# Attention, mixture of experts and a gated second network on one core: maxima in PSUM and three moves in the order of work

## The chip, the core and the metric

The kernel runs on one core of a Trainium2 chip. The metric is the device time of one execution in microseconds (us), lower is better. Every kernel was run several times, and medians are compared; a profile belongs to one more execution, whose own time stands beside its span. The engines are named as in the profile: PE (TensorE, matmuls; PEld is its loading of weights), DVE (VectorE), ACT (ScalarE), POOL (GpSimd), SP (SyncE, which here only issues transfers). SBUF is the core's working memory, PSUM the eight banks that PE writes to.

## The reference

Causal attention over 4 batches, 12 heads, 448 positions of 64 values; its output, as 1792 tokens of 768 values, goes through a layer of 8 experts of which each token uses one, and then through a dense network with h − tanh(h) between its two products.

```python
scores = where(mask, -1e9, q @ k.T / sqrt(64))
x = softmax(scores) @ v                               # 4 x 12 x 448 x 64 -> 1792 x 768
e = argmax(x @ w_gate); gate = softmax(x @ w_gate)[e]
y = gate * sigmoid(x @ w_output_gate)[e] * (relu(x @ w1[e]) @ w2[e])   # 768 -> 1024 -> 768
h = y @ w_in                                          # 768 -> 2048
out = (h - tanh(h)) @ w_out                           # 2048 -> 768
```

## The kernel before

Nothing is scheduled by a planner: each engine works in the order in which the program is written, with waits on the others where data or buffers demand it. Products that need more than 16 bits are split in a high and a low f16 part (`hi`, `lo`).

**Attention** (loop at L610, to about 245 us) goes over 24 units `u` of two heads, each in six pieces `m` of query rows. For a piece PE writes the scores to a PSUM bank with tag "s" (`s_mm`, L323 to L325; three such banks in turn), DVE takes the negated maximum of each row (`s_max`, L333) into an SBUF tile `nm`, multiplies it by 0.125 into `nb` (`s_nb`, L341), and ACT makes exp with `nb` as bias (`s_exp`, L347). A bank is written again when the exp of the piece three before has read it. PE then transposes the result (L365), DVE or ACT copies it out (`t_out`, L371, L373), and PE multiplies with V (L384). Pieces 0 and 1 hold both heads of a unit at once, so that their maxima have two columns; the four others have one. K, Q and V of two units at a time are loaded and split: POOL forms the low parts (L297, L301), and transfers on the SP queue put them in place (L295, L296, L298, L300); POOL issues one load of a pair (L286).

In the units 5 to 15 a chunk `k` of the first expert's raw w1 is converted on the side (`conv1`): ACT makes the high part, POOL the rest, and then `load_raw(1, 0, k)` (L104, SP queue) loads the same chunk of the second expert's w1, 512 KB, in its place.

**The experts** follow, to about 584 us. While the slots of one expert run (`slot`, in steps `z`), the pieces of the next one's weights are converted (`fill_hi`, `fill_lo`; L112, L116, L120). Beside the second expert, `order_a(2)` (L1029, L1037 on DVE) builds an operand and `order_b` (L1056 on PE) multiplies with it, to get the order in which blocks of tokens are handed on.

**The last network** has five groups of token blocks (3, 3, 3, 3, 2). Its loop at L1282 goes over positions `n`, 16 to a group. A position has 18 matmuls (`a_mm`, L1214) into one of two PSUM buffers, then a row of DVE, ACT and POOL operations (`act_a` to `act_d`, L1222 to L1250); the first of these (L1222) empties the buffer. From position 17 on, the second product of the group before runs between them. At n = 9, 10, 11 of group one, the blocks of group two are transposed (`prep2`: PE L148, DVE L150), and right behind each `prep3` makes a small product (PE L1025) that spreads the token scales over the partitions, which ACT copies out (L1026). At n = 12 to 15 SP loads the output weights (`wo_load`, L950); the second of these writes where `prep3`'s operands lie.

Of the kernel before, what the change touches and what calls it, by code (L numbers as in the profile page):

```python
# [12 lines left out]
F32 = mybir.dt.float32  # L13
# [5 lines left out]
ALU = mybir.AluOpType  # L19
AX = mybir.AxisListType  # L20
# [3 lines left out]
B, H, S, D = 4, 12, 448, 64  # L24
# [32 lines left out]
def build(ctx: ExitStack, tc: tile.TileContext, kq0, kq, v, wg, wo, w1, w2, wf, out):  # L57
# [45 lines left out]
    def load_raw(e, x, k, n=1):  # L103
        nc.sync.dma_start(out=(raw1, raw2)[x][:, k : k + n, :], in_=(w1, w2)[x][e, :, k : k + n, :])  # L104
# [73 lines left out]
    with ExitStack() as actx:  # L178
# [133 lines left out]
        def s_mm(u, m):  # L312
            d = st_[u]
            qa, kh, kl = d["t"][0:3]
            hl = (u % 2) * 2
            ps = ps_s.tile([128, 512], F32, tag="s", name=f"s_{u}_{m}")
            i = units[m][0][0]
            n = CP * (i + 1)
            vw = ps[:CP, 0 : len(units[m]) * n].rearrange("p (h n) -> p h n", n=n)
            d["s", m] = vw  # L320
            for z, (_, j) in enumerate(units[m]):
                q = qa[:, hl + j, i * CP : (i + 1) * CP]
                nc.tensor.matmul(out=vw[:, z, :], lhsT=q, rhs=kh[:, hl + j, 0:n], start=True, stop=False)  # L323
                nc.tensor.matmul(out=vw[:, z, :], lhsT=q, rhs=kl[:, hl + j, 0:n], start=False, stop=False)
                nc.tensor.matmul(out=vw[:, z, n - CP : n], lhsT=identb[:CP, :CP], rhs=maskb, start=False, stop=True)  # L325

        def s_max(u, m):
            d = st_[u]
            i, j = units[m][0]
            c0 = 2 * i + j  # L330
            c1 = c0 + len(units[m])
            nm, nb = d["nm"], d["nb"]
            nc.vector.tensor_reduce(out=nm[:, c0:c1], in_=d["s", m], op=ALU.max, axis=AX.X, negate=True)  # L333

        def s_nb(u, m):
            d = st_[u]
            i, j = units[m][0]
            c0 = 2 * i + j
            c1 = c0 + len(units[m])
            nm, nb = d["nm"], d["nb"]  # L340
            nc.vector.tensor_scalar(out=nb[:, c0:c1], in0=nm[:, c0:c1], scalar1=0.125, scalar2=None, op0=ALU.mult)  # L341

        def s_exp(u, m):
            d = st_[u]
# [253 lines left out]
        def conv1(k, z):  # L598
            raw, hi, lo = raw1[:, k], wts0[0][:, 0, k], wts0[0][:, 1, k]
            if z < 2:  # L600
                h = slice(512 * z, 512 * (z + 1))
                scaled("a", hi[:, h], raw[:, h])
            else:
                rest_of("p", lo, raw, hi)
                load_raw(1, 0, k)

        FIRST_T = (NU + 1, 2)
        FILL = {(NU + 1, 4): 1, (NU + 2, 0): 1, (NU + 2, 2): 1, (NU + 2, 4): 1, (NU + 3, 0): 1, 1: 2, 2: 3}
# [2 lines left out]
        for u in range(NU + 5):  # L611
            if ok(u):
                if u % 2 and 3 <= u < 15:
                    load_raw(0, 0, u // 2 - 1)
                if u in (8, 10, 12, 14):
                    load_raw(0, 1, u // 2)
                if u == NU - 2:
                    [load_raw(0, 1, k, 2) for k in range(0, 4, 2)]
                if u == 0:
                    loads[1] = load_unit(1)  # L620
                if u == 1:
                    nc.vector.tensor_scalar(out=wgc[:, :, 0 : 2 * E], in0=wgf, scalar1=WS, scalar2=None, op0=ALU.mult)
                    nc.vector.scalar_tensor_tensor(out=wgc[:, :, 2 * E :], in0=wgf, scalar=WS, in1=wgc[:, :, 0 : 2 * E], op0=ALU.mult,
                                                   op1=ALU.subtract)
                st_[u] = {
                    "t": loads[u // 2][0],
                    "P": at.tile([128, 2, 1120], F32, tag="P", name=f"P_{u}")[:CP],
                    "nm": sm.tile([CP, 8], F32, tag="nm", name=f"nm_{u}"),
                    "nb": sm.tile([CP, 8], F32, tag="nb", name=f"nb_{u}"),
                }  # L630
            if ok(u - 1):
                st_[u - 1]["PT"] = at.tile([CP, 5, 448], F32, tag="PT", name=f"PT_{u - 1}")
            for m in range(6):
                if (u, m) == (0, 5):
                    load_32(2)
                for x, part in zip(START, loads[0][1]):
                    if x == (u, m):
                        part()
                if ok(u) and (m, u % 2) in RS and u // 2 + 1 < 3 * B:
                    loads[u // 2 + 1][1](RS.index((m, u % 2)))  # L640
                if ok(u):
                    s_mm(u, m)
                if m < 5 and ok(u - 1):
                    t_mm(u - 1, m)
                if m == 0 and ok(u - 1):
                    s_exp(u - 1, 5)
                if m > 0 and ok(u):
                    s_exp(u, m - 1)
                if m < 5 and ok(u - 1):
                    t_out(u - 1, m)  # L650
                if m == 5 and ok(u - 3):
                    g_mm(u - 3)
                if m == 1 and ok(u - 4):
                    g_lg(u - 4)
                if ok(u - 2):
                    for z in VM[m]:
                        v_mm(u - 2, *VO[z])
                if ok(u):
                    s_max(u, m)
                if m == 0 and ok(u - 3):  # L660
                    v_out(u - 3, 1, 0)
                if m == 1 and ok(u - 3):
                    v_out(u - 3, 1, 2)
                if m == 3 and ok(u - 2):
                    v_out(u - 2, 0, 0)
                if m == 4 and ok(u - 2):
                    v_out(u - 2, 0, 2)
                if m == 2 and ok(u - 4):
                    g_add(u - 4)
                if m == 2 and ok(u - 3):  # L670
                    x_out(u - 3)
                if m == 3 and NU > u - 3 >= XO:
                    x_store(u - 3)
                if u == 4 and m == 0:
                    wts0 = w_tiles(0)
                if u % 2 and 5 <= u < 17 and 2 <= m < 5:
                    conv1((u - 5) // 2, m - 2)
                for k in CONV.get((u, m), ()):
                    pieces(wts0, [(1, k, *(("a", "v") if k in (2, 3) else ("p", "p")))], 1)
                if u == NU - 1 and m == 0:  # L680
                    t = spare_p("x_first")
                    x_first.extend((t[:, 0 : 2 * DM], t[:, 2 * DM : 2 * DM + F1], t[:, 2 * DM + F1 : 2 * DM + 2 * F1]))
                if (u, m) == FIRST_T:
                    slot_xT(x_first[0], "n0", ps_t)
                    s0 = slot0()
                if (u, m) in FILL:
                    fill0(FILL[u, m])
                if (u, m) == (NU + 2, 0):
                    lctx.close()
                    w16s[1][0] = w16p("w16b1")  # L690
                    wts1 = w_tiles(1, (0,))
                if (u, m) == (NU + 2, 2):
                    w1_next((0,), (0,))
                if (u, m) == (NU + 2, 5):
                    w1_next((1, 2), ())
                if ok(u) and (m, u % 2) == LD and u // 2 + 2 < 3 * B:
                    loads[u // 2 + 2] = load_unit(u // 2 + 2)
                if ok(u):
                    s_nb(u, m)
                if m == 0 and ok(u - 3):  # L700
                    v_out(u - 3, 1, 1)
                if m == 3 and ok(u - 2):
                    v_out(u - 2, 0, 1)
                if ok(u - 4) and (u - 4) % 6 == 5 and m == 2:
                    route = routing((u - 4) // 6)
                if route is not None and (m % 2 == 0 or u >= SLOW):
                    if u - 4 < NU - 1:
                        if next(route) is not None:
                            route = None
                    elif m >= 2:  # L710
                        for weight in route:
                            pass
                        route = None
# [363 lines left out]
    for e in range(E):  # L1077
# [7 lines left out]
        if e + 1 < E:  # L1085
# [10 lines left out]
            def fill_lo(z, e=e):  # L1096
                if e == 0 and z >= 2:
                    next(tl, None)
                pieces(wts[e + 1], PLANS[e][z], e + 2, False)
                if e == 1 and z > 1:  # L1100
                    order_a(z) if z < 3 else order_b()

            fill = (fill_hi, fill_lo)
        else:
# [177 lines left out]
    for n in range(NF + 3):  # L1282
        g, f = divmod(n, KF2)
        if okf(n):
            a_mm(n)
            if n in (9, 10, 11):
                prep2(1, (9, 10, 11).index(n))
                prep3(1, (9, 10, 11).index(n))
            act_a(n)
        if n == 0:  # L1290
            prep1(1, 0, GB[1], False)
# [82 lines left out]
```

## Time and profile before

| | |
|---|---|
| three runs, us | 1056.37, 1058.24, 1058.36 (median 1058.24) |
| the profiled execution, us | 1055.79 |
| its span in the profile, us | 1054.1 |
| mean granted PE clock | 0.982 of full speed |
| busy, us: PE, PEld | 993.4 (94%), 750.0 (71%) |
| busy, us: DVE, ACT, POOL | 801.2 (76%), 597.7 (57%), 471.1 (45%) |
| moved by transfers | 174.93 MB, 166 GB/s over the span |

A timeline row gives the start of an instruction from the beginning of the span, its length, the engine, the line of the program and the operation with its output and inputs; in brackets stands how long the engine was idle before it and whose end it waited for. A row with x18 is 18 such instructions in a row. `DVEq` and `SPq` are the queues' own instructions. Idle time of an engine counts only if a later end hangs on it.

### The profile page before, as it was taken

How to read it: one execution, taken by the hardware profiler on the slowest of the kernel's cores; microseconds unless marked ns; L12 is line 12 of the kernel's file. 1: busy time of each engine (PE TensorE's matmuls, PEld its weight loads, DVE VectorE, ACT ScalarE, POOL GpSimd, SP SyncE). 2: the span in 40 equal slices, each digit the busy share in tenths (PEclk: the TensorE clock that was granted, in tenths of full speed). 3: DMA queues.
4: the chain of work that ended last, by engine and by line, in shares of the span. 5: the costliest groups of instructions: out<-in, count | busy, mean ns of one | idle time of the engine just before them, and what ended most of it. 6: DMA issues, size and time to landing. Idle time of an engine off the chain costs nothing. (4 is left out here: it accounts for less than half of the span.)

```text
span 1054.1 us, 24122 instructions
## 1 busy us (share of the span) xinstructions
PE 993.4 (94%) x9189; PEld 750.0 (71%) x9189; DVE 801.2 (76%) x1609; ACT 597.7 (57%) x1195; POOL 471.1 (45%) x501
## 2 busy tenths in 40 slices
PE   5999999998989999999979879999999999999996
PEld 4999899996867878677856546666666666667763
DVE  7768878786777778778758889888889798786640
ACT  4787776764446266563323578655556566564530
POOL 5476775585111012102227788655544444443321
PEclk9999999999999999999999989999999999999998
DMA  8899998743988878977986605000001000000000
GB/s 246 214 244 298 265 271 210 196 139 113 323 336 302 341 269 321 360 285 251 318 291 231 267 1 215 24 31 23 16 31 38 16 23 16 16 16 16 16 23 23
DMA packets 62833, 174.93 MB, mean 166 GB/s; under 512 B 8400, under 2 KB 23376, under 8 KB 59584
## 3 DMA queue, kind: packets, MB, share of 16 engines
q1 hardware_dynamic: 56352, 147.20, 42.0%
q0 software_dynamic: 6304, 25.63, 8.2%
q8 instruction: 80, 1.31, 0.5%
q14 instruction: 97, 0.79, 0.2%
HBM read 133.09 MB, written 29.62 MB: 154 GB/s over the span
## 5 line engine op out<-in xcount | busy, mean ns | idle before, releaser
L1265 PE MATMUL fo<-wo,g 128*128 128x384 f16 x1344 | 228.2, 326 | 0.0
L1214 PEld LDWEIGHTS <-raw 128*128 128x128 f16 x1440 | 141.8, 99 | 91.2 <-issue 13.7
L1265 PEld LDWEIGHTS <-g 128*128 128x128 f16 x1344 | 131.2, 98 | 83.8
L1224 POOL TENSOR_TENSOR V<-cu,cc 128x384 f32<-128x384 f32 (+1 forms) x80 | 78.8, 985 | 192.5 <-ACT cu L1223 191.8
L161 PEld LDWEIGHTS <-w 128*128 128x128 f16 x2592 | 151.0, 100 | 13.8 <-issue 12.7
L173 PE MATMUL py<-w,hh 128*128 128x384 f16 x544 | 133.8, 328 | 5.6 <-ACT hh L168 5.5
L1214 PE MATMUL fh<-cu,raw 128*128 128x384 f16 (+1 forms) x864 | 134.4, 312 | 4.5 <-DVE cc L1222 4.5
L347 ACT ACTIVATE P<-s,nb 112x112 f32<-112x112 f32 (+1 forms) x192 | 90.2, 496 | 59.3 <-DVE rs L398 29.2
L384 PE MATMUL o<-v,PT 112*112 112x65 f32 x960 | 114.9, 259 | 0.0
L384 PEld LDWEIGHTS o<-v,PT 112*112 112x112 f32 x960 | 105.7, 178 | 0.2 <-ACT xt L406 0.2
L801 POOL DMA_INDIRECT xg<-xs_d,idx x24 | 25.7, 1070 | 173.2 <-issue 38.8
L120 DVE SCALAR_TENSOR_TENSOR w<-raw,w 128x768 f16<-128x768 f32 (+1 forms) x99 | 99.1, 1060 | 2.0 <-ACT w L112 2.0
L112 ACT ACTIVATE w<-raw 128x768 f16<-128x768 f32 (+2 forms) x106 | 89.2, 906 | 16.6 <-ACTq L871 10.4
L1223 ACT ACTIVATE cu<-cc 128x384 f32<-128x384 f32 (+1 forms) x80 | 40.1, 502 | 101.5 <-DVE cc L1222 101.4
L1222 DVE TENSOR_TENSOR cc<-fh,co 128x384 f32<-128x384 f32 (+1 forms) x80 | 42.1, 526 | 68.2 <-PE fh L1214 55.0
L1227 POOL TENSOR_TENSOR X<-cc,X 128x384 f32<-128x384 f32 (+1 forms) x80 | 91.4, 1142 | 4.4 <-ACT cu L1228 0.5
L173 PE MATMUL py<-w,hl 128*128 128x384 f16 x272 | 89.5, 329 | 2.2 <-DVE hl L169 2.2
L333 DVE TENSOR_REDUCE nm<-s 112x2 f32<-112x224 f32 (+1 forms) x144 | 77.2, 536 | 13.5 <-PE s L325 12.1
L1234 DVE SCALAR_TENSOR_TENSOR V<-cu,V 128x384 f32<-128x384 f32 (+1 forms) x80 | 85.2, 1065 | 0.1
L173 PEld LDWEIGHTS <-hh 128*128 128x128 f16 x544 | 52.2, 98 | 38.9 <-ACT hh L168 6.9
L161 PE MATMUL ph<-xT_n,w 128*128 128x128 f16 x1152 | 69.5, 225 | 9.2 <-issue 2.1
L1242 DVE TENSOR_TENSOR V<-V,co 128x384 f32<-128x384 f32 (+1 forms) x64 | 77.8, 1216 | 0.0
(431 smaller groups left out, 1951.1 us busy)
## 6 DMA issues: line engine op xcount, KB each, us to landing
raw<-w SPq DMA_DIRECT2D x48, 512.0 KB
raw<-w SPq DMA_DIRECT2D x60, 384.0 KB
cu<-wf SPq DMA_DIRECT2D x22, 1024.0 KB
wb_d<-co SPq DMA_DIRECT2D x22, 512.0 KB
raw<-kq SPq DMA_DIRECT2D x11, 896.0 KB
ys_d<-yo SPq DMA_DIRECT2D x17, 384.0 KB
raw<-wb_d SPq DMA_DIRECT2D x8, 768.0 KB
xs_d<-xq SPq DMA_DIRECT2D x24, 224.0 KB
```

What stands on the lines that cost most here:

```text
L112: nc.scalar.activation(out=out, in_=in_, func=AF.Copy, scale=WS)
L120: nc.vector.scalar_tensor_tensor(out=out, in0=in_, scalar=WS, in1=hi, op0=ALU.mult, op1=ALU.subtract)
L161: nc.tensor.matmul(out=ph[:, (f % 4) * 128 : (f % 4 + 1) * 128], lhsT=w[0][:, ww, k, f * 128 : (f + 1) * 128], rhs=xTs[tag][:, xx, k, :], ...
L173: nc.tensor.matmul(out=py[:, 0:384], lhsT=hx[:, k, :], rhs=w[1][:, ww, k, z * 384 : (z + 1) * 384], start=(k == 0 and n == 0), stop=(k == ...
L347: nc.scalar.activation(out=d["P"][:, j, OFF[i] : OFF[i] + n], in_=d["s", m][:, z, :], func=AF.Exp, bias=d["nb"][:, 2 * i + j : 2 * i + j + ...
L384: nc.tensor.matmul(out=po[:, i, :], lhsT=d["PT"][:, g, o : o + CP], rhs=d["t"][3][:, hl, j, :], start=(j == 0), stop=(j == i))
L1214: nc.tensor.matmul(out=ph[:, 0:nt], lhsT=wi[ww][:, f // 4, k, f % 4 * 128 : (f % 4 + 1) * 128], rhs=yy[:, k, 0:nt], start=(q == 0), stop=( ...
L1224: nc.gpsimd.tensor_tensor(out=d["V"], in0=d["U"], in1=d["h"], op=ALU.mult)
L1227: nc.gpsimd.tensor_tensor(out=d["X"], in0=d["h"], in1=d["X"], op=ALU.subtract)
L1234: nc.vector.scalar_tensor_tensor(out=d["V"], in0=d[f"S{z}"], scalar=QD[z - 1], in1=d["V"], op0=ALU.add, op1=ALU.mult)
L1242: nc.vector.tensor_tensor(out=d["V"], in0=d["V"], in1=rs_y(g, nt), op=ALU.mult)
L1265: nc.tensor.matmul(out=po[:, 0:384], lhsT=t[:, x, k, i * 128 : (i + 1) * 128], rhs=wo_[ww][:, k, z * 384 : (z + 1) * 384], start=(k == 0 a ...
```

## The change

It has four parts. The row maxima are no longer written to the SBUF tile `nm` but to columns 448 and 449 of the PSUM bank that holds the scores, which these do not use; `s_nb` reads them there. The six loads of the second expert's w1 are issued at the start of units 18 to 23 instead of behind each conversion. `order_a(2)` is written one step of the slot loop sooner. The small products of group two are made at n = 12 (two) and n = 13 (one).

```diff
 def s_mm(u, m):
             d["s", m] = vw
+            d["nm", m] = ps[:CP, S : S + len(units[m])]
 def s_max(u, m):
-            i, j = units[m][0]
-            c0 = 2 * i + j
-            c1 = c0 + len(units[m])
-            nm, nb = d["nm"], d["nb"]
-            nc.vector.tensor_reduce(out=nm[:, c0:c1], in_=d["s", m], op=ALU.max, axis=AX.X, negate=True)
+            nc.vector.tensor_reduce(out=d["nm", m], in_=d["s", m], op=ALU.max, axis=AX.X, negate=True)
 def s_nb(u, m):
-            nm, nb = d["nm"], d["nb"]
-            nc.vector.tensor_scalar(out=nb[:, c0:c1], in0=nm[:, c0:c1], scalar1=0.125, scalar2=None, op0=ALU.mult)
+            nc.vector.tensor_scalar(out=d["nb"][:, c0:c1], in0=d["nm", m], scalar1=0.125, scalar2=None, op0=ALU.mult)
...
 def conv1(k, z):
                 rest_of("p", lo, raw, hi)
-                load_raw(1, 0, k)
...
                 if u in (8, 10, 12, 14):
                     load_raw(0, 1, u // 2)
+                if NU - KD <= u:
+                    load_raw(1, 0, u - NU + KD)
                 if u == NU - 2:
                     [load_raw(0, 1, k, 2) for k in range(0, 4, 2)]
...
-                    "nm": sm.tile([CP, 8], F32, tag="nm", name=f"nm_{u}"),
...
             def fill_lo(z, e=e):
                 pieces(wts[e + 1], PLANS[e][z], e + 2, False)
-                if e == 1 and z > 1:
-                    order_a(z) if z < 3 else order_b()
+                if e == 1 and z in (1, 3):
+                    order_a(2) if z == 1 else order_b()
...
             if n in (9, 10, 11):
                 prep2(1, (9, 10, 11).index(n))
-                prep3(1, (9, 10, 11).index(n))
+            for i in {12: (0, 1), 13: (2,)}.get(n, ()):
+                prep3(1, i)
             act_a(n)
```

NU is 24 and KD is 6. The lines of the changed program stand four lower from L341 on, so L1029 and L1025 below are L1025 and L1021 there.

The queue of SP in the units 21 to 23, before. `xs_d<-xq` stores a unit's result, `raw<-kq` and `raw<-v` load K, Q and V, `kh`, `qa`, `kl` are the copies of their parts, `raw<-w` of 128x1536 the first expert's w2.

```order
L295 DMA kh_3216<-t_11_3219 64x1792 x2
L296 DMA qa_3215<-t_11_3219 64x1792
L298 DMA qa_3215<-lo_3218 64x896
L300 DMA kl_3217<-lo_3218 64x896 x2
L298 DMA qa_3215<-lo_3218 64x896
L300 DMA kl_3217<-lo_3218 64x896 x2
L423 DMA xs_d<-xq_3500 112x4x256
L104 DMA raw_90<-w 128x768
L104 DMA raw_90<-w 128x1536 x2
L423 DMA xs_d<-xq_3664 112x4x256
```

And in the changed kernel:

```order
L295 DMA kh_3192<-t_11_3195 64x1792 x2
L296 DMA qa_3191<-t_11_3195 64x1792
L298 DMA qa_3191<-lo_3194 64x896
L300 DMA kl_3193<-lo_3194 64x896 x2
L104 DMA raw_89<-w 128x1024
L298 DMA qa_3191<-lo_3194 64x896
L300 DMA kl_3193<-lo_3194 64x896 x2
L419 DMA xs_d<-xq_3476 112x4x256
L104 DMA raw_90<-w 128x768
L104 DMA raw_89<-w 128x1024
L104 DMA raw_90<-w 128x1536 x2
L419 DMA xs_d<-xq_3640 112x4x256
```

Two of the loads of 128x1024 are to be seen here, one before the second half of the copies and one between the w2 loads; the rest stands in the same order.

DVE at the end of the second expert's step z = 1, before. `w_2<-raw` are conversions of the next weights, `xT_n` the copy of a transposed slot, `cc` the operand of the ordering matmuls, `order` their result.

```order
L116 TENSOR_SCALAR w_2_8270<-raw_90 128x768
L150 COPY xT_n_85<-pt_I-8512_8513 128x768
L120 SCALAR_TENSOR_TENSOR w_2_8269<-raw_89,w_2_8269 128x1024
L120 SCALAR_TENSOR_TENSOR w_2_8270<-raw_90,w_2_8270 128x768 x3
L1029 TENSOR_TENSOR cc<-pb,io 112x224
L1037 TENSOR_TENSOR cc<-cc,pcs 112x1120
L120 SCALAR_TENSOR_TENSOR w_2_8270<-raw_90,w_2_8270 128x768 x5
L1059 TENSOR_REDUCE smt<-order 128x14
L1060 TENSOR_REDUCE smt<-order 128x14
```

And in the changed kernel:

```order
L120 SCALAR_TENSOR_TENSOR w_2_8245<-raw_89,w_2_8245 128x1024 x4
L1025 TENSOR_TENSOR cc<-pb,io 112x224
L1033 TENSOR_TENSOR cc<-cc,pcs 112x1120
L116 TENSOR_SCALAR w_2_8246<-raw_90 128x768
L150 COPY xT_n_85<-pt_I-8490_8491 128x768
L120 SCALAR_TENSOR_TENSOR w_2_8245<-raw_89,w_2_8245 128x1024
L120 SCALAR_TENSOR_TENSOR w_2_8246<-raw_90,w_2_8246 128x768 x8
L1055 TENSOR_REDUCE smt<-order 128x14
L1056 TENSOR_REDUCE smt<-order 128x14
```

The two rows that write `cc` stand before the conversion and the copy of `xT_n`, and the conversions behind them are in one run.

PE at positions 9 and 10 of the last network, before, one row for each run of matmuls with one output. `pt` are transposes of a block, `rsp` the small product, `fh` the 18 matmuls of a position.

```order
L148 MATMUL pt_I-38658_38659<-identh,wo_34361 128x128
...
L148 MATMUL pt_I-38667_38668<-identh,wo_34361 128x128
...
L1025 MATMUL rsp_I-38676_38677<-wo_34361,onesb 128x256
...
L1214 MATMUL fh_38695<-cu_4971,raw_89 128x384
...
L148 MATMUL pt_I-38714_38715<-identh,wo_34361 128x128
...
L148 MATMUL pt_I-38723_38724<-identh,wo_34361 128x128
...
L1025 MATMUL rsp_I-38732_38733<-wo_34361,onesb 128x256
...
L1214 MATMUL fh_38751<-cu_4971,raw_89 128x384
```

And in the changed kernel, positions 9 to 12:

```order
L148 MATMUL pt_I-38634_38635<-identh,wo_34337 128x128
...
L148 MATMUL pt_I-38643_38644<-identh,wo_34337 128x128
...
L1210 MATMUL fh_38667<-cu_4947,raw_89 128x384
...
L148 MATMUL pt_I-38686_38687<-identh,wo_34337 128x128
...
L148 MATMUL pt_I-38695_38696<-identh,wo_34337 128x128
...
L1210 MATMUL fh_38719<-cu_4947,raw_89 128x384
...
L148 MATMUL pt_I-38738_38739<-identh,wo_34337 128x128
...
L148 MATMUL pt_I-38747_38748<-identh,wo_34337 128x128
...
L1210 MATMUL fh_38771<-cu_4947,raw_89 128x384
...
L1021 MATMUL rsp_I-38790_38791<-wo_34337,onesb 128x256
...
L1021 MATMUL rsp_I-38794_38795<-wo_34337,onesb 128x256
...
L1210 MATMUL fh_38815<-cu_4947,raw_89 128x384
```

Transposes and position matmuls now follow each other, and the first two small products stand together behind position 12's matmuls.

## Rows read from the trace of the kernel before

**Rows 1.** Windows: us, busy of PE PEld DVE ACT POOL, clock, DMA, GB/s.

```profile
55.00:245.00 190.00, 186.24 (x2149) 179.47 (x2147) 151.65 (x477) 140.18 (x342) 131.97 (x151) 1.00 0.84 228
...
637.00:1038.00 401.00, 401.00 (x2630) 253.10 (x2628) 306.26 (x520) 229.60 (x468) 189.55 (x181) 1.00 0.09 32
```

**Rows 2.** Timeline of PE, 21 to 26 us (start, length, operation, [idle, releaser]).

```profile
21.71 0.30 PE L323 MATMUL s<-kh,qa 128*112 128x336 f16 x1 [1.43 <-ACT P L347]
...
23.21 0.35 PE L323 MATMUL s<-kh,qa 128*112 128x448 f16 x1 [0.62 <-ACT P L347]
...
25.29 0.30 PE L323 MATMUL s<-kh,qa 128*112 128x112 f16 x1
```

**Rows 3.** Timelines of DVE, POOL and ACT at the start of attention.

```profile
9.17 0.75 DVE L341 TENSOR_SCALAR nb<-nm 112x2 f32<-112x2 f32 x1
...
19.00 2.02 DVE L341 TENSOR_SCALAR nb<-nm 112x2 f32<-112x2 f32 x1
...
19.12 1.87 POOL L297 TENSOR_TENSOR lo<-raw,t 128x896 f16<-128x896 f32 x1
...
21.05 0.60 ACT L347 ACTIVATE P<-s,nb 112x112 f32<-112x112 f32 x2 [3.27 <-DVE nb L341]
```

**Rows 4.** Groups of DVE to 245 us (busy us, mean ns); one line's semaphores.

```profile
L341 DVE TENSOR_SCALAR nb<-nm 112x2 f32<-112x2 f32 x48 | 26.5, 551 | 1.0
...
L341 DVE TENSOR_SCALAR nb<-nm 112x1 f32<-112x1 f32 x96 | 14.4, 150 | 1.1
...
L395 DVE TENSOR_SCALAR rs<-o 112x4 f32<-112x4 f32 x48 | 7.3, 152 | 1.3 <-PE o L384 1.3
...
L341 DVEq EVENT_SEMAPHORE  x2: 21/21/21, 35.0 to 43.5; - x2
```

**Rows 5.** Timelines of SP's and POOL's transfer issues, 12 to 24 us.

```profile
17.83 0.59 SPq L296 DMA_DIRECT2D qa<-t  x1
...
19.49 1.64 SPq L300 DMA_DIRECT2D kl<-lo  x2
...
22.43 0.60 POOL L286 DMA_DIRECT2D t<-kq  x1 [0.85 <-DMA qa<-t]
```

**Rows 6.** PE, DVE and ACT, 299 to 304 us; window 304 to 306.

```profile
302.64 0.71 PE L1056 MATMUL order<-cc,co 112*128 112x70 bf16 x16 [3.68 <-DVE cc L1037]
...
300.76 0.38 DVE L1029 TENSOR_TENSOR cc<-pb,io 112x224 bf16<-112x224 f32 x1
...
301.25 1.32 DVE L1037 TENSOR_TENSOR cc<-cc,pcs 112x1120 bf16<-112x1120 bf16 x1
...
299.93 0.80 ACT L152 ACTIVATE xT_n<-pt_I-8503_8504 128x768 f16<-128x768 f16 x1
...
304.00:306.00 2.00, 2.00 (x21) 2.00 (x20) 2.00 (x4) 0.78 (x2) 0.00 (x0) 0.50 1.03 420
```

**Rows 7.** Timelines of PE and DVE, 625 to 652 us.

```profile
625.79 0.37 PE L1025 MATMUL rsp_I-38676_38677<-wo,onesb 128*128 128x256 bf16 x1 [3.93 <-DVE yh L150]
...
625.95 5.64 PE L1214 MATMUL fh<-cu,raw 128*128 128x384 f16 x18
...
632.68 3.09 PE L1214 MATMUL fh<-cu,raw 128*128 128x384 f16 x18
...
651.49 0.81 PE L1214 MATMUL fh<-yh,raw 128*128 128x384 f16 x4
...
631.97 0.56 DVE L150 COPY yh<-pt_I-38714_38715 128x768 f16<-128x768 f16 x1 [2.72 <-PE pt_I-38714_38715 L148]
...
647.00 0.55 DVE L1222 TENSOR_TENSOR cc<-fh,co 128x384 f32<-128x384 f32 x1
...
650.42 0.55 DVE L1222 TENSOR_TENSOR cc<-fh,co 128x384 f32<-128x384 f32 x1
```

**Rows 8.** Timeline of SP's issues near 198 us, and of PE at 207 us.

```profile
198.25 1.49 SPq L300 DMA_DIRECT2D kl<-lo  x2
...
207.69 0.21 PE L323 MATMUL s<-kh,qa 128*112 128x112 f16 x1
```

## The prediction

> **What bounds the kernel now.** I read the profile from the outside in. First come the busy times by stage [rows 1]: TensorE (PE) is to be seen at 401.00 of 401 us in the long last stage and at 186.24 of 190 in the body of attention. So a microsecond taken off VectorE (DVE), ScalarE (ACT) or a queue counts only where PE stands still. Next come the orders of time around each place that the edits touch, to find who ended PE's wait there: the start of attention [rows 2, 3], and further down the ordering step of the second expert and the scale products of group two in the last stage. Since PE has no gap from 637 us on, time saved before that stage should reach the end. The profiled execution took 1055.79 us, 2.45 under the median of the three runs (1058.24). I sum against 1055.79 and take the difference from the median. A change under 0.2%, about 2.1 us, can't be told from none.
>
> **Part 1, the row maxima in PSUM.** Of the 144 short multiplications that turn a maximum into the bias of exp, the 96 with one column take 150 ns and the 48 with two columns take 551 ns [rows 4]. One of the long ones is to be seen in [rows 3]: it runs from 19.00 to 21.02, and a GpSimd (POOL) operation runs from 19.12 to 20.99, so both end together; ACT's exp then starts at 21.05 after 3.27 us idle. A DVE operation of nearly the same shape that reads PSUM took 152 ns in each of 48 cases, beside the same POOL work [rows 4]. So I price the new reading at 152 ns: the 19.00 one shrinks by 1.87 us, the 9.17 one by 0.60.
> Writing the maximum to PSUM instead of SBUF has no row of its own. The nearest rows are the short operations of 150 ns, so the bounds are one of these more or less, 0.15 us, 0.9 us over the six reductions of a unit. I take 0, since the reduction works on PSUM already and the 152 and 150 ns lie so close.
> The diff's order also has 78 more semaphore instructions on DVE, 21 ns each [rows 4], 1.6 us in all. They lie beside PE's work: DVE is 151.65 of 190 us busy there [rows 1]. The extra wait of the reductions is for an exp that PE had to wait for before it wrote the same bank, so it has ended.
> What reaches PE: in [rows 2] PE waits 1.43 and 0.62 us for that late exp, and the chain before it may give the 0.60 us of the 9.17 operation. That makes 2.65 us at most, whatever the reductions gain, for PE has no more to give up there. Against it stands the next thing that is late: the copies of the low parts of K for the second pair of units are issued until 21.13, and the nearest copy whose landing shows was issued by 18.42 and landed at 22.43, 4.0 us [rows 5]. If these take as long they land at 25.1, and PE wants them at 25.29 [rows 2], so only 0.2 us would come off; if they take half as long, 2.2. I take 1.5 us, nearer to the short landing because each of these copies is half as large as that one (64x896 against 64x1792 in the orders of the queue), and keep 0.2 to 2.65. In the rest of attention PE is busy 98% of the time, so I take nothing, with 1 us either way.
> [...]
>
> **Part 2, the second expert's first weights.** Six loads of 512 KB leave the places after the conversions of units 5 to 15 and stand at the start of units 18 to 23: on the SP queue the first four go ahead of copies of K and Q, the last two ahead of nothing but weights. Nothing uses them before expert 1. Bytes and instructions stay the same. At 228 GB/s [rows 1] one takes 2.3 us of the transfer engines. The last pair's copies are issued until 199.74, and PE wants the first half at 207.69 [rows 8], 7.95 us later. Two loads (4.6 us) ahead of a copy of up to 4.0 us come to 8.6 in the worst case, 0.7 us over; two pairs, 1.4 us. In the units that the loads leave, each pair carried this much and more, and PE still was busy 98% of the time. I take 0, and keep 1.4 as the bound.
>
> **Part 3, the operand of the ordering step.** Two DVE operations, 0.38 and 1.32 us, move from behind five conversions of weights and a copy of transposes to before them. PE waits 3.68 us for the second of them, until 302.64 [rows 6]. When it no longer waits for DVE, the next to be late is the PSUM buffer, which the ACT copy frees at 299.93 + 0.80 = 300.73. So PE starts 1.9 us sooner. What they are moved past comes 1.7 us later and is for the slots after the ordering matmuls; nothing else waits on DVE there. After the gap PE ran at half its clock (0.50 from 304 to 306), and a shorter gap of 1.8 us may let it fall less. What a whole fall costs is to be seen in [rows 7]: 18 matmuls took 5.64 us instead of 3.09, 2.55 us. Bounds 0 and 2.55; I take 0.8, since the gap is halved and not gone. Together 2.7, bounds 1.9 and 4.45.
>
> **Part 4, the scale products.** PE stands 3.93 us before the first product because DVE, behind two blocks of activation work, has not yet copied the transposes out [rows 7]. Then 18 matmuls take 5.64 us at half clock, so the next transposes come late and DVE waits 2.72 us for them, at 631.97. In the changed order the three products stand two to three positions later, so PE goes from the transposes at 621.9 straight on. The wait of 3.93 and the 2.55 of clock do not both come off: behind them PE is paced by DVE, whose work of one position takes 3.42 us (647.00 to 650.42) against PE's 3.09. The sum goes by DVE: its 2.72 us of waiting vanish, all that follows moves up by that, and the operation at 650.42 comes at 647.70 and ends at 648.25. The matmuls of position 17 need its buffer; they started at 651.49 and may start at 648.25: 3.2 us. The three products cost PE what they did, 0.37 us or less each. Their copies on ACT, two of them now at one position, lie in ACT's waits for DVE, the slower engine; without that cover they would be a rival (below). The load of the output weights on SP that writes where the last product's operand lies is now held until position 13, near 639 (632.68 and two positions); it is wanted behind position 17, 651.49. Bounds: 2.7 (DVE's wait alone) and 3.9 (PE's whole wait). I take 3.2.
>
> **The sum.** 1.5 + 0 + 2.7 + 3.2 = 7.4 us. Against the profiled execution 1055.79 − 7.4 = 1048.4, against the median 1058.24 − 7.4 = 1050.8. With the bounds of the parts the gain is 1.5 to 12 us (least: 0.2 − 0.9 − 1 − 1.4 + 1.9 + 2.7; most: 2.65 + 1 + 4.45 + 3.9).
>
> **The rivals.**
> The start gives nothing, because the copies of the second pair land at 25.1 or because the two-column operation also stalls on PSUM. For it speaks the 4.0 us of [rows 5], against it the 48 readings without a stall [rows 4]. Gain 5.9, time 1052.3.
> In the last stage PE's wait only moves: it waits for DVE position by position, and the later products push back ACT as well, which leaves 0.8 of the 3.2. For it speaks that DVE is the slower of the two there. Gain 5.0, time 1053.2.
> The clock stays up as well at the start, where PE is slowed after its waits; a whole fall there is again 2.55 us. Gain 9.9, time 1048.3.
> The reading of PSUM costs more than that of SBUF. The nearest row that a slower one could follow is 150 against 152 ns, so nothing; a third more, 50 ns, is 0.3 us of the first chain: 1051.1. [...]
> Two of the three gains are swallowed by the next wait: about 2 us are left, 1056.
> **Slower:** the moved loads hold up the last K and Q copies. It decides where these land later than 7.95 us after issue [rows 8]. Were the 4.6 us of two loads exposed whole in both late pairs, with a fall of the clock each time (2.55), that would be 14.3 us lost, less 7.4 gained: 6.9 slower, 1065.1. Against it speaks that the same queue carried the same loads earlier without holding PE.
>
> **How the numbers follow.** Forecast 0.50; the start gives nothing 0.15; the wait only moves 0.12; the clock as well 0.08; dearer PSUM reading 0.03; two swallowed 0.08; slower 0.04. All but the last two are faster by over 0.2%: 0.88. Two swallowed is within 0.2%: 0.08. The predicted time is the forecast's, 1050.8. The range reaches down past the case with the clock (1046.5) and up to just short of two swallowed (1055.5).
>
> **What would show it.** The two-column multiplication in the changed profile means about 150 ns, none at 2 us; the exp at 21.05 comes near 19.2, and the waits of 1.43 and 0.62 us are gone. The ordering matmuls wait under 2 us, released by ACT or by nothing. The scale products wait for nothing; short waits of the position matmuls for DVE appear between 626 and 650, and the 18 matmuls take about 3 us. No wait of PE stands at the first score matmuls of units 20 to 23. It would be wrong if the two-column mean stays near 550, if a wait of several us for a copy of K or Q appears near 190 or 208, or if PE has a gap after 637 us that the old trace has not.

## The result and the profile after

The change took 1047.03 us in the median of 4 runs (1044.79 to 1049.29) against 1058.24 in the median of three of the kernel before; a fourth run of that one, 1075.49 us, was in a slower state and is not compared. The ratio is 0.9899 with a 95% interval of 0.9868 to 0.9930, so 7.4 to 14.0 us less. The forecast was 1050.8, 7.4 us less, with a range of 1046.5 to 1055.5. Two later series gave 0.9910 (0.9875 to 0.9944) and 0.9888 (0.9847 to 0.9930). Single executions of one kernel lie several us apart: 35 of the kernel before, on one chip, went from 1051.43 to 1061.87, and 25 on another from 1053.12 to 1068.26. Much of that goes with PE's clock, 0.990 at the fastest and 0.979 at the slowest of the 35, 0.988 and 0.976 of the 25: whether it falls behind a short gap differs from one execution to the next. Behind a wait of 1.47 us for one exp of attention it stayed at 1.00 in the kernel before; behind 1.79 us for the same exp, in another kernel, it went to 0.50. The profiled execution of the change is the slowest of its four, 1049.29 us with a span of 1047.6.

The windows of the change, with the columns of [rows 1]:

```profile
55.00:245.00 190.00, 189.15 (x2196) 181.82 (x2195) 143.03 (x492) 143.49 (x345) 131.38 (x150) 1.00 0.87 234
...
637.00:1038.00 401.00, 400.32 (x2623) 252.41 (x2621) 300.62 (x511) 224.56 (x459) 185.91 (x177) 1.00 0.09 31
```

PE is busy 189.15 us of the body of attention where it was 186.24, and DVE has 8.6 us less to do there. The last stage is nearly as full as it was: PE stands 0.68 us in it, in two waits of 0.34 us for DVE before the positions 16 and 17. Short waits for DVE were forecast there; a gap after 637 us that the old trace has not was also named as a sign of being wrong, and by the letter these two are that.

The groups of DVE to 245 us, as [rows 4]:

```profile
L337 DVE TENSOR_SCALAR nb<-s 112x1 f32<-112x1 f32 x96 | 14.8, 154 | 1.1
...
L337 DVE TENSOR_SCALAR nb<-s 112x2 f32<-112x2 f32 x48 | 7.6, 159 | 0.9
```

The two-column operation takes 159 ns where it took 551; that is 18.9 us of DVE. The longest of all 144 is 161 ns. The one of unit 1 runs right beside POOL, whose subtraction holds from 19.55 to 21.43 (first DVE, then POOL, then PE and SP, at the start):

```profile
19.58 0.16 DVE L337 TENSOR_SCALAR nb<-s 112x2 f32<-112x2 f32 x1
...
19.55 1.88 POOL L297 TENSOR_TENSOR lo<-raw,t 128x896 f16<-128x896 f32 x1
...
20.67 0.35 PE L324 MATMUL s<-kh,qa 128*112 128x448 f16 x1 [0.41 <-ACT P L343]
...
22.80 0.23 PE L324 MATMUL s<-kh,qa 128*112 128x112 f16 x1 [0.67 <-ACT PT L369]
...
23.52 0.26 PE L325 MATMUL s<-kl,qa 128*112 128x112 f16 x1 [0.50 <-DMA kl<-lo]
...
19.91 1.66 SPq L300 DMA_DIRECT2D kl<-lo  x2
```

Of the waits of 1.43 and 0.62 us of [rows 2], 0.41 is left, and unit 2 begins at 22.80 instead of 25.29. It begins behind a wait of 0.67 for an ACT copy, and then the transfer that was named as next to be late does come late: PE waits 0.50 us for the low part of K, until some 2 us after its issue.

The ordering step and the scale products, on PE:

```profile
296.07 0.70 PE L1052 MATMUL order<-cc,co 112*128 112x70 bf16 x16 [2.10 <-ACT xT_n L152]
...
617.90 0.50 PE L148 MATMUL pt_I-38634_38635<-identh,wo 128*128 128x128 f16 x6
...
619.62 3.09 PE L1210 MATMUL fh<-cu,raw 128*128 128x384 f16 x18 [0.89 <-DVE cc L1218]
...
623.60 3.08 PE L1210 MATMUL fh<-cu,raw 128*128 128x384 f16 x18
...
641.57 2.11 PE L1210 MATMUL fh<-yh,raw 128*128 128x384 f16 x12 [0.34 <-DVE cc L1218]
```

The ordering matmuls wait 2.10 us instead of 3.68 [rows 6], and for ACT. The sign named was a wait under 2 us: this one lies just over it. The position behind the transposes takes 3.09 us instead of 5.64 [rows 7], with a wait of 0.89 in place of 3.93.

### The profile page after: what moved, and what is told of

Same layout as the page of the kernel before. It is cut to its first block, busy times and chain, and to the rows that moved or that the text cites. A ratio compares the mean times of both kernels' runs of the same rounds, so it can differ in the third digit from the quotient of the medians.

```text
span 1047.6 us, 24204 instructions
## 1 busy us (share of the span) xinstructions
PE 991.2 (95%) x9189; PEld 748.4 (71%) x9189; DVE 783.1 (75%) x1609; ACT 596.9 (57%) x1195; POOL 471.3 (45%) x501
## 5 line engine op out<-in xcount | busy, mean ns | idle before, releaser
L1210 PE MATMUL fh<-cu,raw 128*128 128x384 f16 (+1 forms) x864 | 132.1, 308 | 6.6 <-DVE cc L1218 6.6
L330 DVE TENSOR_REDUCE s<-s 112x2 f32<-112x224 f32 (+1 forms) x144 | 78.9, 548 | 15.5 <-PE s L326 14.3
```

The lines of the kernel that those rows point to most:

```text
L330: nc.vector.tensor_reduce(out=d["nm", m], in_=d["s", m], op=ALU.max, axis=AX.X, negate=True)
L1210: nc.tensor.matmul(out=ph[:, 0:nt], lhsT=wi[ww][:, f // 4, k, f % 4 * 128 : (f % 4 + 1) * 128], rhs=yy[:, k, 0:nt], start=(q == 0), stop=( ...
```

## The experiments

All are compared with the kernel before in their own series; ratios of runs are coarse here, so each profile was also measured in stretches, between the starts of the same PE instructions. In the table, A is the start of unit 4; B goes from there to unit 23; C from the first transposes of rows of tokens (L148, at 258.31 before) to the ordering matmuls; D from these to the next second product of an expert; E from the first transposes of group two (621.03 before) to position 16 (648.56). The row "split bias" is the slowest execution of its series.

| kernel | A | B | C | D | E |
|---|---|---|---|---|---|
| before | 42.53 | 174.30 | 44.33 | 10.88 | 27.53 |
| the change | 40.87 | 170.73 | 42.83 | 9.25 | 23.67 |
| part 1 alone | 40.24 | 171.30 | 44.58 | 10.88 | 26.59 |
| part 2 alone | 40.99 | 176.04 | 44.61 | 10.83 | 26.27 |
| part 3 alone | 40.87 | 172.91 | 41.97 | 9.25 | 27.39 |
| part 4 alone | 41.76 | 178.35 | 44.39 | 10.88 | 23.65 |
| all parts, second series | 40.02 | 177.44 | 43.22 | 10.75 | 23.67 |
| all but part 1 | 42.66 | 174.23 | 42.65 | 9.25 | 23.65 |
| split bias | 40.22 | 181.13 | 44.44 | 10.88 | 27.51 |
| all, free bank | 40.38 | 171.62 | 40.45 | 9.25 | 23.65 |
| part 1 to unit 3 | 40.21 | 176.94 | 43.84 | 10.54 | 26.49 |
| part 1 from unit 4 | 41.76 | 178.61 | 43.89 | 12.03 | 26.60 |
| all parts, third series | 39.91 | 171.49 | 41.74 | 9.25 | 23.64 |
| all, free bank, again | 40.32 | 176.31 | 40.48 | 9.25 | 23.65 |

### The four parts, each alone

Each kernel is the one before with the lines of the diff that belong to one part. Part 1:

```diff
+            d["nm", m] = ps[:CP, S : S + len(units[m])]
-            nc.vector.tensor_reduce(out=nm[:, c0:c1], in_=d["s", m], ...)
+            nc.vector.tensor_reduce(out=d["nm", m], in_=d["s", m], ...)
...
-            nc.vector.tensor_scalar(out=nb[:, c0:c1], in0=nm[:, c0:c1], ...)
+            nc.vector.tensor_scalar(out=d["nb"][:, c0:c1], in0=d["nm", m], ...)
```

> Only the row maxima in PSUM. Theory A (the maxima are the whole gain of attention, since the traces of before and after stand 5.1 us apart at the end of attention): 5 us faster than before, 2.5 of it before unit 2 begins and 2.6 in the body, where PE's waits fall from 3.7 us to under 1. Theory B (the moved weight loads give the body's share, by taking work out of units 5 to 15): 2.5 us faster, with PE's waits between 55 and 245 us still near 3.7. The prediction's own term was 1.5 us.

Measured: ratio 0.9981 (0.9956 to 1.0005) over 12 runs, about 2 us, and not clear of nothing. In its profile attention is done 4.9 us sooner, as theory A has it, with PE's waits between 55 and 245 us at 1.5 us; but that is one execution against one, and over the runs the gain is less than half of it.

Part 2:

```diff
-                load_raw(1, 0, k)
+                if NU - KD <= u:
+                    load_raw(1, 0, u - NU + KD)
```

> Only the second expert's first weights loaded late. Theory A and the prediction: no change, within 1 us, with the two-column bias operations still at 550 ns in the mean. Theory B: 2.6 us faster, PE's waits between 55 and 245 us gone. Rival of the prediction: slower, with a wait of PE for copies of K or Q near 190 or 208 us.

Measured: ratio 1.0000 (0.9978 to 1.0023). The two-column bias operations take 646 ns in the mean and PE's waits between 55 and 245 us are 4.0 us, so theory B falls; so does the rival of the prediction, for in none of the profiles with the late loads has PE a wait for copies of K or Q between 185 and 218 us.

Part 3:

```diff
-                if e == 1 and z > 1:
-                    order_a(z) if z < 3 else order_b()
+                if e == 1 and z in (1, 3):
+                    order_a(2) if z == 1 else order_b()
```

> Only the operand of the ordering step built one position sooner. Prediction: 2.7 us faster (1.9 of wait and 0.8 of clock). The traces of before and after show 3.2 us here, 1.6 of it clock, but 1.4 us of that lost again in the next 25 us; a rival is therefore that the gain of clock is only handed on to a later place, and 1.8 us remain.

Measured: ratio 0.9981 (0.9954 to 1.0007). In its profile C is 2.4 us shorter than before and D 1.6; PE waits 1.1 us before the ordering matmuls, for ACT. The gain of clock isn't handed on to a later place: D ends at the first run of second products behind the ordering matmuls, and to the next such run it is 28.4 us here and 30.07 before, 28.2 to 29.9 in the seven profiles with this part and 29.9 to 32.9 in the seven without, 2.4 us less in the mean.

Part 4:

```diff
-                prep3(1, (9, 10, 11).index(n))
+            for i in {12: (0, 1), 13: (2,)}.get(n, ()):
+                prep3(1, i)
```

> Only the scale products of group two moved. Prediction: 3.2 us faster, from DVE's 2.72 us of waiting and the slack behind it; PE at full clock from 624 to 632 us and 18 matmuls in 3.1 us. Rival: the wait only moves to DVE, 0.8 us faster.

Measured: ratio 0.9969 (0.9937 to 1.0000). E is 23.65 us, in all seven profiles with this part 23.6 to 23.7, and 26.3 to 27.5 in the seven without. Not all of that lasts: position 17 starts 3.43 us behind position 16, with a wait for DVE, where it was 2.93. From the first transposes of group two to the end of the execution it is 429.7 us in all seven with the part and 431.8 to 433.1 in the seven without, 2.8 less in the mean. So the rival, 0.8, falls too. The ratios of the four parts add up to 0.69% less, 7.3 us.

### All parts again, and all but the first

> All four parts, once more and with more runs. If the parts add up as they were measured alone (1.0, 0 and two times about 2 to 3 us), 7 us faster than before, ratio 0.993. If they help each other, as the first measurement of the change says (11 us), ratio 0.990.

Measured: 1050.19 against 1058.23, ratio 0.9910 (0.9875 to 0.9944). Its interval holds both expected values, so this doesn't settle whether the parts help each other. Its profile shows what scatters. Windows at the end of unit 9, with the columns of [rows 1]:

```profile
92.00:94.00 2.00, 0.50 (x4) 0.10 (x2) 1.93 (x7) 1.02 (x3) 1.92 (x4) 1.00 0.83 271
94.00:96.00 2.00, 1.33 (x11) 1.33 (x12) 0.15 (x1) 0.46 (x1) 1.89 (x4) 0.53 0.79 195
96.00:98.00 2.00, 2.00 (x16) 2.00 (x16) 0.32 (x2) 0.98 (x2) 1.83 (x3) 0.50 0.87 172
```

Two waits for POOL's `xq` (1.16 and 1.01 us) stand before a stretch at half clock. Units 9 and 10, which take 8.88 and 9.14 us undisturbed, took 12.39 and 11.09.

The change without its first part is the diff less the lines shown for part 1.

> The change without its first part (maxima in SBUF as before). Theory A, the maxima give 5 us at the end of attention and these are kept to the end: 5 us slower than all four parts together, 3 to 5 us faster than before. Theory B, what attention gains is given back among the experts: within 2 us of all four parts.

Measured: ratio 0.9932 (0.9906 to 0.9957), 7.2 us faster than before and 2.3 slower than all parts in the same series by the ratios. That lies near theory B's edge and speaks against the 5 us of theory A, but the two intervals overlap. Here and in part 1 alone the maxima are worth some 2 us in the whole kernel, and in neither is that clear of nothing.

### What stalls: the form in SBUF

```diff
-            nc.vector.tensor_scalar(out=nb[:, c0:c1], in0=nm[:, c0:c1], scalar1=0.125, ...)
+            for c in range(c0, c1):
+                nc.vector.tensor_scalar(out=nb[:, c : c + 1], in0=nm[:, c : c + 1], scalar1=0.125, ...)
```

> The kernel before, with each two-column bias operation made as two of one column, all in SBUF. Theory A, the stall belongs to the form with two columns in SBUF on both sides: no bias operation over 200 ns, and attention ends about 4 us sooner, though 48 more operations run. Theory C, the stall belongs to any operation of SBUF that runs beside POOL, so that PSUM is what helps: still operations of over 500 ns among them, and attention no shorter.

Measured: ratio 0.9942 (0.9905 to 0.9980). The line's own answer for the bias operations (shortest, median and longest in ns):

```profile
L342 DVE TENSOR_SCALAR nb<-nm x192: 142/153/156, 8.9 to 231.5; 112x1 f32<-112x1 f32 x192
```

None of the 192 stalls, all in SBUF: theory C falls, and the stall belongs to the form with two columns. A is 40.22 us, as short as with PSUM. The expected gain of attention, though, isn't in this profile, which is the slowest execution of its twelve (1062.06 us, the median is 1052.26): B is 181.13, with two units of 11.52 and 14.67 us instead of 8.88 and 9.07, and PE at half clock from 120 to 128 us. Over the runs this kernel is 6.1 us faster than before (2.1 to 10.1), where part 1 alone gave 2.0 (from 0.5 slower to 4.7 faster). The intervals overlap, so it isn't shown that either form is the better one.

### Where part 1 gains: the start or the body

Against part 1 alone:

```diff
-            d["nm", m] = ps[:CP, S : S + len(units[m])]
+            d["nm", m] = ps[...] if u < 4 else d["nm"][...]      # the other kernel: u >= 4
```

> The kernel before, with the maxima in PSUM in units 0 to 3 alone. If the start gives 1.4 us by itself (units 4 begin at 40.4 us in the mean with the maxima in PSUM, at 41.8 without), unit 4 begins near 40.4 us here, and from there to unit 23 it takes 172 us or more as without them, with waits of PE for exp in the units 9 to 20.

> The kernel before, with the maxima in PSUM from unit 4 on alone. Unit 4 begins near 41.8 us as without them. Theory A, the short operations of the body cost PE 2 to 4 us that the prediction set at nothing: unit 4 to unit 23 in about 171 us, unless PE's clock falls once. Rival, the body's length is scatter alone: 172 to 178 us.

Measured: 0.9977 (0.9939 to 1.0015) and 0.9976 (0.9937 to 1.0015). The start is as expected: A is 40.21 with the maxima in PSUM in units 0 to 3, and 41.76 without. The body of the first kernel is as expected too: B is 176.94, with waits of PE for exp of 1.35 and 0.39 us. That of the second is not: from unit 4 on with PSUM, B is 178.61. Both forms stand in one profile of the second kernel:

```profile
L338 DVE TENSOR_SCALAR nb<-s 112x2 f32<-112x2 f32 x40 | 6.4, 159 | 0.7
L338 DVE TENSOR_SCALAR nb<-nm 112x2 f32<-112x2 f32 x8 | 5.8, 726 | 0.3
```

What held PE in this body (DVE, POOL and PE, then the windows):

```profile
104.83 2.40 DVE L505 TENSOR_SCALAR pi<-pi 112x4 int32<-112x4 int32 x1
...
105.32 1.89 POOL L297 TENSOR_TENSOR lo<-raw,t 128x896 f16<-128x896 f32 x1
...
109.26 0.30 PE L325 MATMUL s<-kh,qa 128*112 128x336 f16 x1 [1.79 <-ACT P L344]
...
110.00:112.00 2.00, 2.00 (x15) 1.86 (x13) 1.90 (x9) 2.00 (x9) 0.79 (x2) 0.58 0.94 326
112.00:114.00 2.00, 2.00 (x13) 2.00 (x12) 1.17 (x4) 1.62 (x4) 1.97 (x3) 0.50 0.21 56
```

An integer operation of the routing, with four columns in SBUF, ends with POOL at 107.2 after 2.40 us; the exp behind it is late, PE waits 1.79 us and then runs at half clock, and the unit, 11, takes 14.23 us. The change leaves these operations as they are. So theory A of the body isn't shown: with PSUM in the body B is 173.9 us in the mean of seven profiles, without 175.5 in six (split bias left out), and one fall of the clock is worth more than that. One unit hints at more than scatter: this unit 11 takes 10.2 to 13.7 us in all seven profiles with the maxima in SBUF there, and 8.9 to 9.1 in five of the seven with them in PSUM. It was picked out afterwards from nineteen units, and unit 17 leans the other way, so it shows nothing yet.

### The ordering matmuls in a free bank

```diff
-        px = mp_t.tile([128, 512], F32, tag="t", name="order")[:, 0 : 5 * NBLK]
+        px = mp_h.tile([128, 512], F32, tag="s", name="order")[:, 0 : 5 * NBLK]
```

> All four parts, and the ordering matmuls write to a bank of the pool of the first product that is free there, so that they need not wait for the copy by ACT. Theory A: their wait of 2.10 us goes, and about 2 us come off all four parts (more where the clock fell behind that wait). Rival: the wait moves to the next matmuls, which need ACT's copies too, and nothing comes off.

> All four parts, a third time, beside the next kernel: ratio 0.990 to 0.991.

> All four parts and the ordering matmuls in the free bank, again: no wait before them, and 2 to 3 us less than all four parts in the same series, ratio near 0.988.

Measured: 1047.03 beside 1050.19 of all four parts in one series, 1048.22 beside 1048.52 in the next; ratios to the kernel before 0.9891 (0.9846 to 0.9936) and 0.9899 (0.9861 to 0.9938), where all four parts had 0.9910 and 0.9888. In the profile the wait is gone:

```profile
294.21 0.70 PE L1052 MATMUL order<-cc,co 112*128 112x70 bf16 x16
```

and C is 40.45 and 40.48 us, 2.0 less than the 42.48 of the five profiles that have part 3 with the old bank. In the whole time the 2 us can't be told from nothing, so this version isn't shown to beat the change.

## Why the prediction was right

**The maxima.** The price of the bias operation was right, 159 ns against 152, and the extra waits and the writing to PSUM cost nothing that shows: the reductions take 10 to 13 ns more, inside the 0.15 us of the bounds. The reductions of pieces 1 in the kernel before, and in the changed one:

```profile
L333 DVE TENSOR_REDUCE nm<-s 112x2 f32<-112x448 f32 x24 | 14.7, 613 | 0.0
```

```profile
L330 DVE TENSOR_REDUCE s<-s 112x2 f32<-112x448 f32 x24 | 14.9, 623 | 0.0
```

The rival in which reading PSUM costs 50 ns more doesn't show: the one-column operation went from 150 ns, reading SBUF, to 154, reading PSUM.

The term of the start, 1.5 us, was right in size: A is 40.28 us in the mean of seven profiles with PSUM at the start and 41.76 in six without (split bias left out). The cap that was named, the copies of K's low parts, works twice: PE waits for one 0.50 us at unit 2 and for another 0.71 at 32.46, so that of the 2.49 us by which unit 2 begins sooner 1.66 are left at unit 4. But one term of the chain was missed, and the size is in part luck. The operation on DVE just before the reduction of the 19.00 one, from 16.67 on, had stalled beside POOL as well. Its groups before and in the change:

```profile
L623 DVE SCALAR_TENSOR_TENSOR wgc<-wgf,wgc 128x96 f16<-128x96 f32 x1 | 2.0, 1991 | 0.0
```

```profile
L620 DVE SCALAR_TENSOR_TENSOR wgc<-wgf,wgc 128x96 f16<-128x96 f32 x1 | 0.3, 259 | 0.0
```

The change doesn't touch it. It comes at 16.17 there, ahead of POOL's subtraction at 17.09, and the exp that was to come near 19.2 comes at 17.14. In the six profiles without PSUM at the start unit 2 begins three times at 25.29 to 25.72, in two of them behind 1.99 and 1.96 us of this operation, and three times at 23.37 to 23.85; with PSUM it begins at 22.05 to 22.80, in the change behind 0.26 us.

The body of attention, taken as 0 ± 1, can't be settled: 1.5 us by the means, less than one fall of the clock with its gap (3 to 6 us in a unit).

**The loads.** 0 was right: the part alone gives 1.0000, and in no profile with the late loads does a unit from 20 to 23 wait for a copy.

**The ordering step.** Of the 2.7 us, 1.9 stood for the wait and 0.8 for the clock. The wait: C is 42.48 us in five profiles and 44.30 in the seven without the part, 1.8 less, and ACT's copy of `xT_n` is what PE waits for, as the prediction had it. The clock was the mis-sized half: D is 9.25 us in four of the five and 10.75 in the one where the wait was 3.06, against 10.99 in the mean without, so 1.4 us. Behind the waits of 1.08 to 2.10 us, in four profiles, the clock stayed up (1.00 in the change's); behind those of 3.06 and 3.68 us it fell to half (0.50). Together 3.3.

**The scale products.** 3.2 us were forecast, from DVE's own pace, with position 17 at 648.25. Counted from the same transposes it comes at 648.12, 3.4 us sooner than in the trace that the sum was made from, and that is kept to the end (3.37 us). So the reading was right. That trace is the one with the longest E of the seven without the part, though: in the mean of seven profiles each, E is 23.65 against 26.91 us, and to the end of the execution 2.8 us are left. The short waits for DVE that were to appear are there (0.89, 0.34).

**The sum.** 1.5 + 0 + 3.3 + 2.8 = 7.6 us by the stretches, 7.3 by the four parts alone, each of which is known to some 3 us only; forecast were 7.4. The whole change gave 10.7, with an interval that begins at 7.4, and 9.5 and 11.9 in the later series. So the three places and their sizes were right, while the forecast total lay at the low end of what was measured. What lies between may be the body of attention or scatter; the runs don't tell.

## What to carry to other kernels

Price a small operation that is slow only now and then by what runs beside it: where its end falls together with another engine's, moving one operand or changing its shape is worth a try, and one row of a like operation elsewhere in the trace says what it should cost. When two waits are chained, sum by the engine that sets the pace behind them, not by the longest wait; and measure the gain to the end, for here half a microsecond went again one position on. And where PE's clock falls after gaps, compare stretches of several profiles: the whole time of one part alone was not clear of nothing here, while the stretches C and E told parts 3 and 4 apart in every profile.

## What the runs showed of the hardware

The stall beside POOL depends on the form. With SBUF on both sides, two columns took up to 2.18 us before, and 726 ns in the mean of the eight that were left in one kernel; 24 of the 48 before took over 0.2 us, and each of these ended 0.02 to 0.03 us after a POOL operation. One column took 0.15 us in each of 96 cases before, and 156 ns at most in the 192 of the split form; two columns read from PSUM took 161 ns at most in the change. Other operations of DVE with SBUF on both sides stalled as well: 96 columns of `wgc` took 1.99 us instead of 0.26, four integer columns 2.40. I had priced PSUM alone as the way out, and the split operations show that it is not the only one. Why the form decides, no row shows.

A fall of PE's clock behind a gap cost 1.6 us beside the ordering step (10.88 against 9.25), and with its gap 3 to 6 us in a unit of attention (12.39, 14.23 and 14.67 us instead of about 9). It came in some executions of the same kernel and not in others: of the three profiles of the change, one has D at 10.75 and unit 9 at 12.39 us, the two others D at 9.25 and unit 9 at 9.24 and 8.88. Much of the scatter of the single times goes with it: of the change itself, the four executions had clocks of 0.993, 0.992, 0.987 and 0.985 at 1045.89, 1044.79, 1048.17 and 1049.29 us.
